# An S4D convolution by matmuls: the spectra's product in a form chosen by block, the skip term by four 32x32 products, a third buffer for one factor of the kernel rows, and an order of the work read from a table

## The chip, the core and the metric

The kernel runs on one core of a Trainium2 chip. The core has five engines with a queue of instructions each: TensorE (PE in the profile, its weight loads apart as PEld), VectorE (DVE), ScalarE (ACT), GpSimd (POOL) and SyncE (SP), which issues transfers here. Each queue runs in its written order and waits at its head by semaphores. The metric is the device time of one execution in microseconds, lower is better.

## The reference

One layer over 2048 tokens of 640 channels: an adaptive layer norm, a long convolution by a diagonal state space model (S4D), a gated sum, a second norm and a SwiGLU feed-forward network (FFN) of 1728 hidden channels.

```python
def _A_ref(u, log_A_real, A_imag, C_real, C_imag, log_dt, D_skip):
    dt = jnp.exp(log_dt)
    A = -jnp.exp(log_A_real) + 1j * A_imag                 # [640, 128]
    C = (C_real + 1j * C_imag) * dt[:, None]
    P = jnp.exp((A * dt[:, None])[:, :, None] * pos)       # pos = 0 .. 2047
    K = 2.0 * jnp.einsum("dn,dnl->dl", C, P).real          # one kernel row a channel
    y = irfft(rfft(u, 2 * L) * rfft(K, 2 * L))[:L]         # along the tokens
    return y + u * D_skip

mod = (_silu(c) @ w_mod).reshape(1, 6, 1, -1)
sa, ca, ga, sb, cb, gb = ...
h = _layernorm(x) * (1 + ca) + sa
x = x + ga * _A_ref(h, ...)
h = _layernorm(x) * (1 + cb) + sb
x = x + gb * ((_silu(h @ w1) * (h @ w3)) @ w2)
```

## The kernel before

**Stages.** The channels are cut into five blocks b = 0 .. 4 of 128. For each block the kernel makes the convolution's kernel rows, transforms them and the normalized input, multiplies the spectra, transforms back and stores the result (`zd`). When all five blocks are done, rows of 128 tokens are read back from `zd` (`iz`, `izb`), the last step of the inverse transform adds them to x (`iy`, `iyb`), and the second norm, the transposes (`tp`) and the FFN follow (`gu` are the first gate and up products, then `acc`, `c`, `X`). The change does not touch the FFN's own code (`ffn`, L1412, and what it calls).

**Kernel rows** (`gen_chunk`, L594; tasks in `gen_tasks`, L1739). A block has eight chunks c of 16 channels, named `g{b}.{c}`. A chunk runs: on POOL a phase `ph` and three sizes z0, z1 (two halves of `yy`) and z2 (half of `xx`), from the tables `p` and the exponents `e` and `late` (made by ACT in `exp_tasks`, L1933, from the products `al` x `j`); on ACT one Abs on `ph` and four sines `tr`; on DVE five products m0 to m4 that complete `yy` and `xx`; on PE 32 matmuls of 32 columns, four side by side in the array (`kps`); on ACT a copy of the result into `ks` (task r); on DVE the sum of the skip term D into position 63 of each row of `ks` (task d, `skip`, L1761). `yy` and `xx` have two buffers each, `kps` one PSUM tile of two halves that alternate, `tr` three PSUM tiles.

**Transforms and product.** A first transform is a task m of eight matmuls into one PSUM bank, eight such tasks a block for the kernel rows (`ps<-wk,ks`) and eight for the input (`ps<-wk,xb`) (`first_tasks`, L1812); its moving matrix `wk` has two zero blocks of 64x64. ACT or DVE copies each bank to `sp` or `sp2`. The second transform makes half tiles i = 0 .. 7 of the spectra, `fh` of the input and `fk` of the kernel, eight matmuls each (`spectra_tasks`, L1850). ACT holds `fh` in SBUF as `hz`. DVE multiplies complex numbers: `fp = fk * re(hz)`, `fk = fk * im(hz)`, both of 512 elements a partition, and then one difference and one sum of 256 (`both`, L1879). Two half tiles make one `fp`, and `inverse` (L1886) makes of it two banks `fz` with two matmuls each, whose copies `zt` go to `zd`.

**The normalized input.** `h_tasks` (L1793) normalizes tokens into `hn` (on ACT or DVE), multiplies and adds rows into `hb` on DVE, stores it (`hs`) and reads it back turned as `xb`.

**The order.** All tasks up to the first hidden tiles are recorded with the tasks that they follow, the rings of buffers that they take and give, and one or two engines that may run them (`Plan`, L168). `place` (L188) then walks the tasks as a list scheduler with modelled durations and delays; ties go by a table `RANKS` of one number a task. The result is the order of each engine's queue. Every instruction passes through a helper that keeps this order (`InOrder`, whose line is L157 for all of them), so the trace tells instructions apart by tile and shape, not by line.

Of the kernel before, what the change touches and what calls it, by code (L numbers as in the profile page):

```python
# [29 lines left out]
EXPS = ((0, 0, 0, 64.0), (0, 1, 0, 1.0), (1, 0, 0, 512.0), (1, 1, 4, 8.0), (1, 2, 0, 8.0))  # L30
# [3 lines left out]
RANKS = """  # L34
# [132 lines left out]

class Plan:  # L168

    LAG = dict(PE=0.2, DVE=0.18, ACT=0.2, POOL=0.15, SP=0.0)
    CHAIN = dict(DVE=0.12, ACT=0.12, POOL=0.07)
# [2002 lines left out]
```

## Time and profile before

| | |
|---|---|
| median of three runs | 973.44 us (972.19 to 976.54) |
| profiled execution | 972.31 us |
| its span | 970.5 us |
| its mean granted TensorE clock | 0.975 |
| DVE, last product of a kernel row ends | 342.5 us |
| PE, last `kps` ends | 346.4 us |
| PE, first `gu` in the chain that ended last | 398.07 us |

Times in the views are microseconds from the start of the span. Rows of groups give the engine, the operation, the result's tile and the operands' tiles (buffer numbers left out), partitions x elements, the count, then busy time and the mean duration in ns, then the idle time of that engine just before them and the engine and tile that ended it. An fp32 matmul leaves two records, so 32 matmuls of `kps` are 64; a few records are missing here and there. In the chain of waits each piece is what the next one waited for.

### The profile page before, as it was taken

How to read it: one execution, taken by the hardware profiler on the slowest of the kernel's cores; microseconds unless marked ns; L12 is line 12 of the kernel's file. 1: busy time of each engine (PE TensorE's matmuls, PEld its weight loads, DVE VectorE, ACT ScalarE, POOL GpSimd, SP SyncE). 2: the span in 40 equal slices, each digit the busy share in tenths (PEclk: the TensorE clock that was granted, in tenths of full speed). 3: DMA queues.
4: the chain of work that ended last, by engine and by line, in shares of the span. 5: the costliest groups of instructions: out<-in, count | busy, mean ns of one | idle time of the engine just before them, and what ended most of it. 6: DMA issues, size and time to landing. Idle time of an engine off the chain costs nothing.

```text
span 970.5 us, 20551 instructions
## 1 busy us (share of the span) xinstructions
PE 859.9 (89%) x7985; PEld 681.8 (70%) x7985; DVE 702.0 (72%) x1395; ACT 546.4 (56%) x1022; POOL 340.5 (35%) x371
## 2 busy tenths in 40 slices
PE   1464787889899997899999999999999999999997
PEld 1132665767778884677777778888788888888775
DVE  7998899999999968886767677557456464645422
ACT  6877788979888851564434455346444344443412
POOL 1797889879799600002111111000011212120000
PEclk9996999999999999799999999999999999999999
DMA  9955453723425268935434422276342322220374
GB/s 218 275 168 191 111 136 95 177 66 106 111 80 152 74 159 206 241 118 182 122 120 139 122 96 68 82 209 194 112 134 64 102 77 86 82 82 28 108 220 133
DMA packets 110506, 127.31 MB, mean 131 GB/s; under 512 B 10568, under 2 KB 90696, under 8 KB 109128
## 3 DMA queue, kind: packets, MB, share of 16 engines
q1 hardware_dynamic: 109032, 125.21, 45.3%
q8 instruction: 63, 1.03, 0.5%
q10 hardware_dynamic: 1376, 0.79, 0.3%
q14 instruction: 35, 0.29, 0.1%
HBM read 95.82 MB, written 30.15 MB: 130 GB/s over the span
## 4 chain that ended last, share of the span: by engine, by line
PE 70%; DVE 17%; ACT 5%; issue 4%; DMA 3%; POOL 1%; SPq 1%; ACTq 0%; DVEq 0%
PE c L157 19%; PE acc L157 18%; PE X L157 12%; PE ps L157 4%; PE gu L157 3%; DVE yy L157 3%; PE kps L157 3%; PE fz L157 2%; PE fk L157 2%; DVE fp L157 2%; PE fh L157 2%; DVE hn L157 2%; DVE xx L157 2%; DVE xb L157 1%; ACT tr L157 1%
## 5 line engine op out<-in xcount | busy, mean ns | idle before, releaser
L157 PE MATMUL acc<-ah,w 128*128 128x512 f32 x560 | 173.2, 395 | 2.4 <-DMA w<-w2d 1.7
L157 PEld LDWEIGHTS acc<-ah,w 128*128 128x128 f32 x560 | 103.7, 188 | 26.4 <-issue 2.1
L157 PE MATMUL acc<-al,w 128*128 128x512 f32 x260 | 102.4, 394 | 0.0
L665 DVE TENSOR_TENSOR wl<-s,wh 128x256 fp32r<-128x256 f32 x92 | 38.9, 423 | 67.5 <-ACT wh L664 67.1
L841 POOL TENSOR_TENSOR s<-wr 128x256 f32<-128x256 f32 x22 | 16.4, 744 | 187.8 <-DMA wr<-in_w 94.8
L157 POOL TENSOR_TENSOR ph<-p,p 128x1024 int32<-128x1024 int32 x40 | 79.2, 1979 | 8.2 <-ACT tr L157 8.0
L664 ACT ACTIVATE wh<-s 128x256 fp32r<-128x256 f32 x92 | 37.6, 410 | 78.5 <-PE X L157 58.1
L157 PE MATMUL kps<-yy,xx 128*32 128x64 f32 x2560 | 51.8, 234 | 28.6 <-DVE xx L157 21.4
L157 DVE TENSOR_TENSOR yy<-yy,tr 128x512 f32<-128x512 f32 (+1 forms) x80 | 75.3, 943 | 1.2 <-ACT tr L157 0.6
L157 PEld LDWEIGHTS kps<-yy,xx 128*32 128x32 f32 x2560 | 45.1, 116 | 38.3 <-issue 22.0
L664 ACT ACTIVATE wh<-wr 128x256 fp32r<-128x256 f32 x92 | 38.4, 418 | 56.0 <-PE X L157 42.3
L842 POOL TENSOR_TENSOR s<-s,wr 128x256 f32<-128x256 f32 x22 | 16.6, 755 | 134.0 <-issue 133.9
L902 ACT ACTIVATE t<-g 128x512 f32<-128x512 f32 x44 | 27.8, 632 | 52.7 <-DVE g L866 52.7
L157 ACT ACTIVATE tr<-ph,hpi 128x512 f32<-128x512 f32 x80 | 54.6, 690 | 4.4 <-DVE xx L157 2.7
L157 PEld LDWEIGHTS acc<-al,w 128*128 128x128 f32 x260 | 48.9, 188 | 10.8 <-DVE al L665 0.3
L871 DVE SCALAR_TENSOR_TENSOR g<-t,g 128x512 f32<-128x512 f32 x48 | 33.7, 702 | 31.3 <-ACT t L902 29.3
L157 POOL TENSOR_TENSOR yy<-e,e 128x512 f32<-128x512 f32 x48 | 52.4, 1109 | 8.8 <-PE kps L157 5.9
L157 DVE TENSOR_TENSOR xx<-tr,xx 128x512 f32<-128x512 f32 x80 | 54.3, 680 | 1.1 <-ACT tr L157 1.1
L157 PE MATMUL ps<-wk,ks 128*64 128x128 f32 x640 | 42.4, 285 | 13.6 <-DVE ks L157 8.9
L157 ACT ACTIVATE tr<-ph 128x512 f32<-128x512 int32 x80 | 47.3, 598 | 12.4 <-DVE yy L157 6.5
L157 PE MATMUL ps<-wk,xb 128*64 128x128 f32 x640 | 46.1, 295 | 6.3 <-ACT sp L157 3.0
L157 PEld LDWEIGHTS ps<-wk,ks 128*64 128x64 f32 x640 | 37.0, 143 | 20.3 <-ACT hn L157 6.6
(448 smaller groups left out, 2379.7 us busy)
## 6 DMA issues: line engine op xcount, KB each, us to landing
w<-w2d SPq DMA_DIRECT2D x42, 640.0 KB, 3.9
wr<-in_w SPq DMA_DIRECT2D x50, 320.0 KB, 3.9
zd<-zt SPq DMA_DIRECT2D x40, 256.0 KB, 2.9
w2d<-w SPq DMA_DIRECT2D x14, 640.0 KB, 3.5
xs<-in_x SPq DMA_DIRECT2D x16, 320.0 KB, 11.3
hs<-hb SPq DMA_DIRECT2D x20, 256.0 KB, 2.5
xb<-hs SPq DMA_DIRECT2D x20, 256.0 KB, 4.9
iz<-zd SPq DMA_DIRECT2D x32, 160.0 KB, 5.0
```

The costliest lines, as they stand in the source:

```text
L157: self.prev = self.k.order(f(*a, **kw), self.prev)
L664: self.nc.scalar.activation(H, v, AF.Copy)
L665: eng.tensor_tensor(Lo, v, H.bitcast(F32), op=ALU.subtract)
L841: eng.tensor_tensor(s[0], u[:, 0:2], u[:, 2:4], op=ALU.add)
L842: eng.tensor_tensor(s[1], s[0], g[:, 0:2], op=ALU.subtract)
L871: V.scalar_tensor_tensor(g, th, 1.0, g, op0=ALU.add, op1=ALU.mult)
L902: tanh = lambda o, i: A.activation(o, i, AF.Tanh, scale=0.5)
```

## The change

**The spectra's product** has a form for each block, `FORM = "AABBC"`. B is the form of before. A is one DVE instruction for a half tile, all four products of 1024 elements a partition, into an `fp` of twice the size; the difference and the sum are left to PSUM, with a third matrix in `wz` and eight matmuls for a tile of `fz` where there were four. C is the one product, then the difference and the sum from SBUF, and gives the bank of `fk` free before these.

**The skip term** is four matmuls of 32x32 with the identity, on top of `kps`; task d and its DVE instruction are gone. Each `kps` is a PSUM tile of its own in a ring of one.

**The first transform** skips the zero blocks of `wk`: eight columns of the input take 32 matmuls in the four quadrants of the array, into two banks; four tasks a block for eight.

**Buffers and tables.** Each third chunk of blocks 0 to 3 takes its `yy` in `x2[0]`, named `x_94` in the trace, which nothing uses until later. The products for the exponents are made in the exponents' own tile, on POOL in all five blocks. `iz` tiles 0 and 1 use `sp2`.

**The order** is a table of task numbers (an apostrophe chooses the second engine) that `sequence` reads and checks against the tasks and the rings; the model is gone. The tasks' durations, now used by nothing, changed too.

```diff
-EXPS = ((0, 0, 0, 64.0), (0, 1, 0, 1.0), (1, 0, 0, 512.0), (1, 1, 4, 8.0), (1, 2, 0, 8.0))
+EXPS = ((0, 0, 0, 64.0), (1, 0, 0, 512.0), (1, 1, 4, 8.0), (1, 2, 0, 8.0), (0, 1, 0, 1.0))
-RANKS = """
--1152 -1540 -1534 -1515 -1509 -1417 -1345 -1436 -1412 -1402 -1385 -1330 -1273 -1351 -1452 -1478 -1480 -1475 -1459 -1510 -1507
...
+ORDER = """
+1 78 80 81 82 83 79 150 2 20 19 21 86 22 23 84 42 41 5 4 43 44 24 25 45 46 14 111 15 16 17 47 18 30 26 8 27 107 48 49 31 100 50 61
...
+FORM = "AABBC"
-    wz = np.tile(np.stack([np.block([c, s]), np.block([-s, c])], 1), (2, 1, 1))
+    wz = np.tile(np.stack([np.block([c, s]), np.block([-s, c]), np.block([-c, -s])], 1), (2, 1, 1))
...
+        for x in ORDER.split():
+            n = names[int(x.rstrip("'"))]
+            engs, _, _, after, _, _, take, give, _, _ = T[n]
+            assert n not in done and done.issuperset(after), n
...
+            out.append((engs[x.endswith("'")], n))
...
+    def in_third(self, b, c):
+        return b < NB - 1 and (8 * b + c) % 3 == 2
+
+    def third(self):
+        return self.x2[0].rearrange("p j d -> p (j d)")[:, :2048].rearrange("p (r d a i) -> p r d a i", r=2, d=self.CD, a=2)
...
-        yy = w.tile([P, 2, C, 2, 32], F32, name=f"yy_{d0}", tag="yy")
+        yy = self.third() if self.in_third(d0 // P, d0 % P // C) else w.tile([P, 2, C, 2, 32], F32, name=f"yy_{d0}", tag="yy")
...
+            for q in range(4):
+                g = slice(32 * q, 32 * q + 32)
+                nc.tensor.matmul(kps.rearrange("p (e b) -> p e b", b=64)[g, :, 63], self.ident[g, g], self.dsk[g, d0 // P, d0 % P // 4:d0 % P // 4 + 4],
+                                 start=False, stop=True, skip_group_check=True, tile_position=(32 * q, 32 * q))
...
-                if b == c == 0:
-                    self.kg = self.psg.tile([P, 2, 256], F32, name="kps", tag="kg", bufs=1)
-                kps[c] = self.kg[:, c % 2]
+                kps[c] = self.psg.tile([P, 256], F32, name=f"kps{b}{c}", tag="kg", bufs=1)
...
-        def skip(c):
-            o = slice(4 * c, 4 * c + 4)
-            V.tensor_add(self.ks[b][:, o, 63], kps.pop(c).rearrange("p (e b) -> p e b", b=64)[:, :, 63], self.dsk[:, b, o])
...
-            for e in range(4):
-                x = self.ks[b][:, 4 * i + e, :] if m else xb[:, :, 4 * i + e]
+            for e in range(8):
+                x = self.ks[b][:, 8 * i + e, :] if m else xb[:, :, 8 * i + e]
                 for r in range(2):
-                    o = pk[i][r * 64:(r + 1) * 64].rearrange("p (v j i f) -> p i j v f", j=4, i=4, f=2)[:, e]
-                    nc.tensor.matmul(o, x, self.wk[:, r, :], start=True, stop=True, tile_position=(0, 64 * r))
+                    for h in range(2):
+                        g = slice(64 * h, 64 * h + 64)
+                        o = pk[i, h][r * 64:(r + 1) * 64].rearrange("p (v j i f) -> p i j v f", j=2, i=8, f=2)[:, e]
+                        nc.tensor.matmul(o, x[g], self.wk[g, r, g], start=True, stop=True, tile_position=(64 * h, 64 * r))
...
+            if form == "B":
+                k = bank[1, i]
+                for r in range(2):
+                    nc.vector.tensor_mul(k if r else prod[i // 2][:, 0, :, o, :].rearrange("p r q d -> p q r d"), k, bc(held[i][:, :, r], 2, 2))
+                return
+            k = bank.pop((1, i)).rearrange("p q r d -> p r (q d)")
+            h = held[i].rearrange("p q r d -> p r (q d)")
+            to = prod[i // 2][:, :, :, o, :].rearrange("p s r q d -> p s r (q d)")
+            nc.vector.tensor_mul(to, bc(k, 1, 2), bc(h, 2, 2))
...
+            terms = ((0, 0, 0), (0, 1, 1), (1, 1, 2), (1, 0, 1))[:2 if last else 4]
...
+            for n, (s, r, w) in enumerate(terms):
                 for f in range(2):
                     g = slice(64 * f, 64 * f + 64)
+                    nc.tensor.matmul(bank["z", j, f], self.wz[g, w, :], p[g, s, r], start=(n == 0), stop=(n == len(terms) - 1), tile_position=(64 * f, 0))
...
+            x[0] = E[0][:, :, 1, :]
             self.eng(e).tensor_tensor(x[0], bc(self.al[:, b], 2, 8), bc(self.j8, 1, P), op=ALU.mult)
```

How the queues stand, at three places. First DVE while the kernel rows of the second block are made, where the products of the first block's spectra stand between the products of the chunks (`yy`, `xx`) and the normalization (`hn`, `hb`). Before:

```order
L157 TENSOR_TENSOR fp_1507<-fk_1482,hz_1473 128x2x2x128
L157 SCALAR_TENSOR_TENSOR yy_1469<-yy_1469,tr_192_1492 128x16x32
L157 TENSOR_TENSOR fk_1482<-fk_1482,hz_1473 128x512
L157 TENSOR_TENSOR fp_1507<-fk_1514,hz_1524 128x2x2x128
L157 TENSOR_TENSOR fp_1507<-fp_1507,fk_1482 128x256 x2
L157 TENSOR_TENSOR fk_1514<-fk_1514,hz_1524 128x512
L157 TENSOR_TENSOR yy_1469<-yy_1469,tr_192_1492 128x16x32
```

Now:

```order
L149 TENSOR_TENSOR fp_1492<-fk_1478,hz_1487 128x4x256
L149 TENSOR_TENSOR xx_1444<-tr_160_1461,xx_1444 128x512
L149 TENSOR_TENSOR hb_1495<-hn,rw 128x512
L149 SCALAR_TENSOR_TENSOR yy_1445<-yy_1445,tr_160_1447 128x16x32
L149 TENSOR_TENSOR hn<-hn,rw 128x512
L149 TENSOR_TENSOR hb_1573<-hn,rw 128x512
L149 TENSOR_TENSOR fp_1492<-fk_1552,hz_1566 128x4x256
```

The four rows of a half tile (two products, a pair of sums) are one row with the product of 1024 elements, and nothing follows it on DVE.

Second PE at the end of the kernel rows, from the last two chunks on. Before:

```order
L157 MATMUL kps<-yy_4463,xx_4462 32x64 x32
L157 MATMUL ps_4787<-wk,ks_4131 64x4x16x2 x8
L157 MATMUL ps_4798<-wk,ks_4131 64x4x16x2 x8
L157 MATMUL kps<-yy_4582,xx_4581 32x64 x32
L157 MATMUL ps_4841<-wk,ks_4131 64x4x16x2 x8
L157 MATMUL ps_4878<-wk,ks_4131 64x4x16x2 x8
L157 MATMUL ps_4892<-wk,ks_4131 64x4x16x2 x8
L157 MATMUL ps_4912<-wk,ks_4131 64x4x16x2 x8
L157 MATMUL fh_4926<-sp,wb 64x128 x8
```

Now (the last two rows alternate, sixteen of each, to the end of the task, and `fh` follows them):

```order
L149 MATMUL kps_5523<-yy_5290,xx_5289 32x64 x32
L149 MATMUL kps_5523<-dsk,ident 32x4 x4
L149 MATMUL kps_5570<-yy_5439,xx_5438 32x64 x32
L149 MATMUL kps_5570<-dsk,ident 32x4 x4
L149 MATMUL ps_5610<-wk,ks_4792 64x2x16x2
L149 MATMUL ps_5611<-wk,ks_4792 64x2x16x2
```

The four rows `dsk,ident` are the skip term. The last two chunks stand side by side, and one task of the first transform stands behind the last of them, where four stood.

Third POOL in the second block. Before, each chunk's sizes go into one of two buffers `yy`:

```order
L157 TENSOR_TENSOR ph_1089<-p_119,p_120 128x1024
L157 TENSOR_TENSOR yy_1091<-late 128x16x32
L157 TENSOR_TENSOR xx_1090<-late 128x512
L157 TENSOR_TENSOR yy_1091<-late 128x16x32
L157 TENSOR_TENSOR ph_1169<-p_119,p_120 128x1024
L157 TENSOR_TENSOR xx_1170<-late 128x512
```

Now the block's first chunk has its sizes in `x_94`, and the product for a later block's exponents is on POOL (its last row here):

```order
L149 TENSOR_TENSOR ph_1087<-p_119,p_120 128x1024
L149 TENSOR_TENSOR x_94<-late 128x16x32
L149 TENSOR_TENSOR xx_1088<-late 128x512
L149 TENSOR_TENSOR x_94<-late 128x16x32
L149 TENSOR_TENSOR ph_1305<-p_119,p_120 128x1024
L149 TENSOR_TENSOR yy_1307<-late 128x16x32 x2
L149 TENSOR_TENSOR xx_1306<-late 128x512
L149 TENSOR_TENSOR ph_1443<-p_119,p_120 128x1024
L149 TENSOR_TENSOR yy_1445<-late 128x16x32 x2
L149 TENSOR_TENSOR ph_1451<-p_119,p_120 128x1024
L149 TENSOR_TENSOR xx_1444<-late 128x512
L149 TENSOR_TENSOR e_122<-al,j_110 128x128x8
```

In these rows the sizes go to three different buffers in turn, and POOL has one instruction of 1024 elements more.

More of the change, by code (lines that the diff above doesn't have):

```diff
@@ L168 @@
 class Plan:
-    LAG = dict(PE=0.2, DVE=0.18, ACT=0.2, POOL=0.15, SP=0.0)
-    CHAIN = dict(DVE=0.12, ACT=0.12, POOL=0.07)
-    NEAR, RATE, LAND, FLY, ISSUE, AWAY, TABLE = 0.1, 235e3, 1.3, 0.7, 0.06, 8, 1.28
     def __init__(self, **rings):
@@ L258, in place @@
+        taken, done, out = {r: [] for r in self.n}, set(), []
+        for x in ORDER.split():
+            n = names[int(x.rstrip("'"))]
+            engs, _, _, after, _, _, take, give, _, _ = T[n]
+            assert n not in done and done.issuperset(after), n
+            for r, y, _ in take:
+                i = len(taken[r]) - self.n[r]
+                assert i < 0 or not uses[r, taken[r][i]], n
+                taken[r].append(y)
             for k in give:
                 uses[k] -= 1
-                given[k] = max(fin + self.LAG.get(e, 0.0), given.get(k, 0.0))
@@ L261, in place @@
-                if not uses[k]:
-                    freed[k] = given[k]
-            for m in nexts[n]:
-                left[m] -= 1
-                if not left[m]:
-                    ready.append(m)
-        assert len(end) == len(T), ("never", [n for n in T if n not in end][:20])
-        return order
-    def run(self):
-        T = self.tasks
-        found = [int(x) for x in RANKS.split()]
-        searched = [n for n in T if n not in self.own]
-        assert len(found) == len(searched)
-        self.order = self.place({n: t[4] for n, t in T.items()} | dict(zip(searched, found)))
-        for s, f, e, n in self.order:
-            if T[n][2]:
-                T[n][2](e)
+            done.add(n)
@@ L282 @@
+            out.append((engs[x.endswith("'")], n))
+        assert len(done) == len(T)
+        return out
+    def run(self):
+        for e, n in self.sequence():
+            if self.tasks[n][2]:
+                self.tasks[n][2](e)
 class K:
@@ L1113, in dst @@
                         return z[u][pr][h * 64:h * 64 + 64]
-                    load(f"iz{u}.{pr}{h}", zv[:, t0:t0 + 2, :cut], dst, 262144, done + ([f"hh{b4}.{i}.m" for i in range(8)] if u > 2 else []))
+                    load(f"iz{u}.{pr}{h}", zv[:, t0:t0 + 2, :cut], dst, 262144, done + ([f"hh{b4}.{i}.m" for i in range(4)] if u > 2 else []),
+                         "inv" if u < 2 else "change")
         def load_up(m):
@@ L1613, in border @@
             self.x2 += [self.fp.tile([P, 4, D], F32, name=f"x2{i}") for i in (2, 3)]
-        plan.add("change", None, 0, change, [f"g{b}.7.p", f"g{b}.7.d"] + [f"h{b}.{i}.x" for i in range(4)], 0, own=True)
+        plan.add("change", None, 0, change, [f"g{b}.7.p", f"g{b}.7.r"] + [f"h{b}.{i}.x" for i in range(4)], 0, own=True)
         self.tail_tasks(border, cut)
@@ L1787, in gen_tasks @@
                     give=[("tr", n + f"s{(0, 0, 1, 3, 4)[i]}")])
-            add(n + "p", "PE", 1.1, lambda c=c: ch[c][4](), [n + f"m{i}" for i in range(5)], t + 3,
-                take=[("kg", 1)], give=[("yy", n + "z0"), ("xx", n + "z2")])
-            add(n + "r", "ACT", .27, lambda c=c: rows(c), [n + "p"] + ([f"k{b - 1}.{i}.m" for i in range(8)] if b else ["exp0", "q0.t0", "q1.t0"]), t + 3, give=[("kg", n + "p")])
-            add(n + "d", "DVE", .1, lambda c=c: skip(c), [n + "r"] + (["dsk"] if b == 0 else []), t + 3, give=[("kg", n + "p")])
+            add(n + "p", "PE", 1.25, lambda c=c: ch[c][4](), [n + f"m{i}" for i in range(5)] + (["dsk"] if b == 0 else []), t + 3,
+                take=[("kg", 1)], give=[(yy, n + "z0"), ("xx", n + "z2")])
+            add(n + "r", "ACT", .27, lambda c=c: rows(c), [n + "p"] + ([f"k{b - 1}.{i}.m" for i in range(4)] if b else ["exp0", "q0.t0", "q1.t0"]), t + 3, give=[("kg", n + "p")])
     def h_tasks(self, b):
@@ L1855, in spectra_tasks @@
         bank, prod, held = {}, {}, {}
-        four = lambda x: x.rearrange("p (q r d) -> p q r d", q=2, r=2)
+        form = FORM[b]
+        last = form != "A"
+        four = lambda x: x.rearrange("p (r q d) -> p q r d", q=2, r=2)
         def of(m, i):
@@ L2035, in early_tasks @@
         for b in range(4):
-            add(f"x{b}", "SP", 0, lambda b=b: load_xs(b), [], next(lp), dma=[327680] * 4, take=[("xs", 1)])
+            add(f"x{b}", "SP", 0, lambda b=b: load_xs(b), [], next(lp), dma=[360000] * 4, take=[("xs", 1)])
         for k in range(5):
@@ L2086, in scale @@
             self.h_rs = self.rsqrt(self.gp, self.h_ss, NJ, "h", (self.h_nm, 1.0), 1.0 / D, [t[:, i * NJ:(i + 1) * NJ] for i in range(2)])
-        add("hscale", "DVE", 6.5, scale, [f"mean{b}" for b in range(4)] + [f"sq{b}{j}" for b in range(4) if b not in W["stat_v"] for j in range(4)], W["stat"](4), take=[("f2", 1)])
+        add("hscale", "DVE", 5.5, scale, [f"mean{b}" for b in range(4)] + [f"sq{b}{j}" for b in range(4) if b not in W["stat_v"] for j in range(4)], W["stat"](4), take=[("f2", 1)])
         add("hscalef", None, 0, None, ["hscale"], give=[("f2", "hscale")])
@@ L2095, in rows_begin @@
             A.activation(m[:96, 384:], pm[0][:96, 384:], AF.Copy)
-        add("m", "ACT", .9, rows_begin, ["mr4"], 20, take=[("hz", 4)])
+        add("m", "ACT", .6, rows_begin, ["mr4"], 20, take=[("hz", 4)])
         pr = {}
@@ L2117, in fold @@
             V.tensor_mul(self.rB, self.rB, self.rows[2])
-        add("fold", "DVE", 1.6, fold, [f"rw{g}" for g in range(4)], 22, port=True)
+        add("fold", "DVE", 3.2, fold, [f"rw{g}" for g in range(4)], 22, port=True)
         add("wb", "SP", 0, lambda: nc.sync.dma_start(self.wb, self.t_wb), ["fold", "mr4", "lat1", "turn1"], 60, dma=[2097152])
```

270 lines of the change are left out of this document (121 added, 149 removed), and 80 rows, old and new, of tables (ORDER, RANKS).

## The prediction

> **What bounds the kernel now.** I read the page first: its busy totals, its slices, its chain.
>
> ```profile
> PE 859.9 (89%) x7985; PEld 681.8 (70%) x7985; DVE 702.0 (72%) x1395; ACT 546.4 (56%) x1022; POOL 340.5 (35%) x371
> PE   1464787889899997899999999999999999999997
> DVE  7998899999999968886767677557456464645422
> POOL 1797889879799600002111111000011212120000
> PE 70%; DVE 17%; ACT 5%; issue 4%; DMA 3%; POOL 1%; SPq 1%; ACTq 0%; DVEq 0%
> ```
>
> A slice is 24 us. In the first fourteen (to about 340 us) DVE stands at 8 or 9 and PE below it for long; behind them PE alone stands at 9. Averages hide two programs, so the second view is busy time by stretches (us, then PE, PEld, DVE, ACT, POOL busy with their counts, granted clock, DMA share, GB/s): the convolution's generation of rows, its end, the first gated tiles, and the FFN's rest.
>
> ```profile
> 105.50:342.50 237.00, 207.26 (x4226) 173.90 (x4228) 226.74 (x418) 198.72 (x339) 202.51 (x198) 0.97 0.42 110
> 342.50:398.10 55.60, 46.35 (x594) 34.31 (x583) 42.92 (x128) 20.09 (x38) 0.63 (x1) 0.89 0.81 197
> 448.90:970.50 521.60, 511.87 (x2284) 407.71 (x2283) 299.16 (x593) 220.68 (x447) 62.51 (x84) 1.00 0.37 114
> 171.20:236.40 65.20, 56.01 (x1120) 46.81 (x1118) 62.77 (x119) 56.21 (x95) 56.69 (x57) 0.95 0.43 114
> 291.50:342.50 51.00, 49.78 (x1052) 42.15 (x1050) 48.86 (x88) 42.68 (x76) 39.43 (x34) 1.00 0.42 115
> ```
>
> From 448.9 us on PE is busy 511.87 of 521.60 us, and the change doesn't touch that code: 522 us stand. From 105.5 to 342.5 us DVE is busy 96% and PE 87%. So DVE sets this stage, with PE behind it; in its last block (291.5 to 342.5) PE is busy 49.78 of 51.00 and the two are level. What is taken from DVE is worth its full size only as long as PE and POOL have room.
>
> **The change part by part.** Instructions on DVE overlap a little, so I cost them by the distance between starts, from the timeline (start, duration, engine, instruction):
>
> ```profile
> 303.37 0.15 DVE L157 TENSOR_TENSOR ks<-kps,dsk 128x4 f32<-128x4 f32 x1
> 303.69 1.22 DVE L157 TENSOR_TENSOR yy<-yy,tr 128x1024 f32<-128x1024 f32 x1 [0.17 <-ACT tr L157]
> 304.83 0.68 DVE L157 TENSOR_TENSOR fp<-fk,hz 128x512 f32<-128x512 f32 x1
> 305.44 0.68 DVE L157 TENSOR_TENSOR xx<-tr,xx 128x512 f32<-128x512 f32 x1
> 306.59 0.17 DVE L157 TENSOR_TENSOR ks<-kps,dsk 128x4 f32<-128x4 f32 x1 [0.47 <-ACT ks L157]
> 306.67 0.69 DVE L157 TENSOR_TENSOR fk<-fk,hz 128x512 f32<-128x512 f32 x1
> 307.98 0.74 DVE L157 TENSOR_TENSOR fp<-fp,fk 128x256 f32<-128x256 f32 x2
> 308.64 0.68 DVE L157 TENSOR_TENSOR fp<-fk,hz 128x512 f32<-128x512 f32 x1
> ```
>
> 512 elements take 0.60 us of the queue (304.83 to 305.44), 1024 take 1.14 (303.69 to 304.83), a pair of 256-element sums 0.66 (307.98 to 308.64). *Products.* A half tile i of the spectra costs 0.60 + 0.60 + 0.66 = 1.86 us on DVE now. Form A, in blocks 0 and 1, is one product of 1024: no row has one with a factor in PSUM. From below it is the 1.14 of `yy<-yy,tr`, from above two products of 512, 1.20; I take 1.16, so 0.70 less for each of 16 half tiles: -11.2 us. Form C, in block 4, makes 1.86 into 1.14 + 0.66: next to nothing.
>
> The other edits on DVE, by groups of equal instructions up to 342.5 us (busy and mean ns, then idle time before them and its releasers):
>
> ```profile
> L157 DVE TENSOR_TENSOR ks<-kps,dsk 128x4 f32<-128x4 f32 x38 | 5.7, 157 | 5.6 <-PE kps L157 3.1 <-ACT ks L157 1.3 <-ACT hn L157 1.1
> L157 DVE TENSOR_SCALAR hn<-xq,rs_y_h,rs_n_h 128x128 f32<-128x128 f32 x44 | 18.1, 412 | 1.2
> L157 DVE COPY sp<-ps 128x512 f32<-128x512 f32 x19 | 12.7, 682 | 2.5 <-PE ps L157 2.3
> L157 DVE COPY zt<-fz 128x512 f32<-128x512 f32 x5 | 3.4, 684 | 0.8 <-PE fz L157 0.7
> L157 DVE TENSOR_TENSOR xs_al<-al,j 128x1024 f32<-128x1024 f32 x1 | 2.8, 2835 | 0.0
> L157 DVE TENSOR_TENSOR ks<-al,j 128x1024 f32<-128x1024 f32 x1 | 1.2, 1216 | 0.0
> ```
>
> The skip adds go: of their 0.157 some 0.10 is the queue's own (306.59 to 306.67 is the least), so 38 make -3.8, and their 5.6 us of idle can go too. The two exponent tables go to POOL: -4.0. The table moves 16 pieces of the first normalization to ACT, -16 x 0.40 = -6.4, and back to DVE 12 copies of the first transform and 5 of the inverse: 17 x 0.61 = +10.4. Sum on DVE: -11.2 - 3.8 - 4.0 - 6.4 + 10.4 = **-15.0 us**, before any idle time.
>
> *PE* pays for it. Its groups up to 346.4 us, two rows of its weight loads, and pieces of the chain of waits (start, length):
>
> ```profile
> L157 PE MATMUL kps<-yy,xx 128*32 128x64 f32 x2560 | 51.8, 234 | 28.6 <-DVE xx L157 21.4 <-POOL xx L157 2.9 <-ACT sp L157 2.4
> L157 PE MATMUL ps<-wk,xb 128*64 128x128 f32 x640 | 46.1, 295 | 6.3 <-ACT sp L157 3.0 <-ACT zt L157 1.4 <-DVE fp L157 1.4
> L157 PEld LDWEIGHTS kps<-yy,xx 128*32 128x32 f32 x2560 | 45.1, 116 | 38.3 <-issue 22.0 <-POOL xx L157 4.0 <-POOL yy L157 3.0
> L157 PEld LDWEIGHTS ps<-wk,xb 128*64 128x64 f32 x640 | 42.5, 220 | 10.9 <-ACT sp L157 4.4 <-issue 3.0 <-ACT zt L157 2.3
> ```
> ```profile
> 306.13 1.06 PE fh L157 x16
> 307.19 0.91 PE fk L157 x16
> 325.08 1.10 PE kps L157 x61
> 326.18 1.92 PE fz L157 x8
> 345.29 1.10 PE kps L157 x61
> 346.39 3.64 PE ps L157 x64
> 364.36 0.74 DVE fp L157 x2
> ```
>
> An fp32 matmul leaves two records. *Inverse.* Four more matmuls for each of 8 tiles of form A: 8 x 1.92 = +15.4 us (326.18), in the second and third block, where PE has room (busy 56.01 of 65.20 in 171 to 236 us). *Skip term.* Four matmuls are 8 records; at the 1.10 us of 64 `kps` records they are 0.14, from above four whole `kps` durations, 0.94. A change of shape shows at 306.13: `fh` behind `kps` takes 1.06 and the `fk` after it 0.91, so 0.15. I take 0.15 for each chunk, near the low end, since the four go to different quarters of the array: 34 chunks after 105.5 us, +5.1; with a change of shape on either side of them it is 0.30, +5 more. The Trainium skill, "TensorEngine Tiling (Array Packing)", Key Properties, says that a change of tiling mode drains the engine; the trace agrees with its 0.15, and by that rule PE's sum below would be +14. *First transform.* Eight columns now take 32 quadrant matmuls, 64 records like a `kps` task, where they took 32 records of twice the width. For the kernel rows that was 3.64 / 2 = 1.82 us (346.39); at the `kps` rate it is 1.10, or 2.2 if the 64-column load, twice as wide, is what counts. I take 1.10 (the streamed width, 64, is that of `kps`): 4 tasks x 4 blocks x -0.72 = -11.5. For the input's half the loads are the longest, 220 ns against 116, and fill 42.5 of 46.1 us; I leave it at its present cost, bounds -15 (at the `kps` rate) and +2. Sum on PE: +15.4 + 5.1 - 11.5 = **+9**, so 216 us of work in a stage that would last 222.
>
> *POOL and ACT.* The third buffer goes against POOL's waits, shown for 34 to 342 us with total, number and longest; the tables cost POOL two rows more:
>
> ```profile
> POOL yy L157 <- PE kps L157: 14.9, 11, 3.9
> POOL ph L157 <- ACT tr L157: 8.0, 6, 3.0
> L157 POOL TENSOR_TENSOR al<-al,j 128x1024 f32<-128x1024 f32 x3 | 5.9, 1971 | 0.0
> L157 ACT ACTIVATE ks<-kps 128x256 f32<-128x256 f32 x38 | 14.3, 379 | 10.5 <-PE kps L157 9.3 <-DVE ks L157 0.8
> L157 ACT ACTIVATE ph<-ph 128x1024 f32<-128x1024 int32 x40 | 42.2, 1055 | 0.4
> ```
>
> +2 x 1.97 = +3.9 us in POOL's queue, hidden by its 34 idle us (202.51 busy of 237), which shrink by the 15 the stage is to lose and, at best, by these 14.9. One `kps` buffer for two makes each `kps` wait for ACT's copy of the chunk before; a copy is 0.38, and ACT was idle before it waiting for PE (9.3 us), so it follows its `kps` at once and PE has other tasks in between. I take 0, from above the copy and its signal each time, some 0.6 x 34 = 20 us.
>
> *Sum.* The stage ends at 342.5 - 15.0 + 0.5 = 328: the idle before the skip adds (5.6) goes, and I give as much and 0.5 more to a PE and a POOL that are nearly full. Its end: behind the last `kps` stand one new transform task, not four old ones (1.10 for 3.64, -2.5); the last two `kps` are neighbours and share a buffer, +0.6; form C moves two sums off PSUM (such a pair stands in the chain at 364.36), -0.5. So -2.4. The profiled execution took 972.31 (span 970.5 and 1.8 around it): 972.31 - 14.5 - 2.4 = 955.4. It lay 1.1 below the median of the runs, 973.44, so I predict **956**.
>
> **The rivals.**
> *POOL takes over* (to 966). Its waits for `kps` were 11 with up to 3.9 us; if the third buffer, used for each third chunk alone, takes away half (7.5) and the tables add 3.9, its last phase moves by 4 us, not 15. With the tail: -6.4. Against it: POOL was busy only 85% of the stage.
> *PE takes over through weight loads* (to 969). If a 64-column load lasts as long with half the rows, a new task is 64 x 0.034 = 2.2 us, the kernel rows' half costs +6, not -11.5, the input's +2; PE then has 207 + 15 + 5 + 8 = 235 us, and the stage ends near 340: -2.5, tail -1. For it: `PEld` is busy 45.1 of `kps`'s 51.8. Against: 128-row loads of 64 columns go in 1.82 / 32 = 0.057 with N = 128, so streaming sets that row. The Trainium skill has the rule for this rival: "TensorE: Matmul & The Clock Gate", LDWEIGHTS (loading the stationary operand), counts a load by its columns and not by its rows.
> *Slower: the single `kps` buffer* (987). `kps` waits at the head of PE's queue until ACT has come to the copy, with transforms and inverses behind it; ACT is busy 84% of the stage (198.72 of 237). PE has 222 - 216 = 6 us to spare; a wait of w for 34 chunks adds 34w - 6. The whole gain of 17 is gone from w = 0.68 on, and at 1.1 us it is +31 - 17 = +14: 987. For it: a `ph` row of 1.055 us may stand ahead of such a copy. Against: the 9.3 us above.
> *No gain* (972). A new order puts waits where DVE was freed; the transfers between the last spectrum and the first inverse row are untouched either way.
>
> **How the numbers follow.** Forecast 0.56 (its own range 947 to 963: products 1.20 and skip at 0.30 above, the input's half at the `kps` rate and the idle gone below). POOL 0.11, PE 0.12, single buffer 0.12, no gain 0.09. A measurement here tells about 0.5% (4.9 us) from no change. Faster: 0.56 + 0.11, half of PE's, and 0.02 of no gain: 0.75. Same: the other half and 0.04: 0.10. Slower: 0.12 + 0.03 = 0.15. The range goes from 940, below the forecast's own by the rest of PE's and DVE's idle, to 974, which leaves out the buffer's case and some ends.
>
> **What would show it.** Products of 1024 at about 1.2 us and no `ks<-kps,dsk` on DVE; `fz` chains of 3.8 us in two blocks; a quadrant task of the kernel rows near 1.1 us (2.2 speaks for PE's rival); POOL's waits on `kps` well below 14.9; the last `kps` done near 332 (before: 346.4) and `gu` some 17 us earlier. `kps` waiting for ACT's `ks` by more than 0.6 us a chunk would make the prediction wrong, as would PE idle time that DVE no longer explains.

## The result

The changed kernel is slower by 0.7%.

| kernel | median us | runs | ratio to before, 95% interval |
|---|---|---|---|
| before | 972.9 (971.1 to 976.9) | 9 | |
| changed | 981.7 (975.3 to 984.7) | 9 | 1.0074 (1.0044 to 1.0103) |
| predicted | 956 (940 to 974) | | |

The profiled execution of the changed kernel took 983.58 us, 11.3 more than that of before. Its page, the busy totals, two of the slices and the transfers of instructions (queue, kind, number, MB, share):

```profile
PE 871.1 (89%) x9649; PEld 685.0 (70%) x9649; DVE 686.3 (70%) x1292; ACT 548.4 (56%) x1026; POOL 344.2 (35%) x376
PE   1355787899998979699999999999999999999997
DVE  7889789889996958888677767657465564646322
q8 instruction: 76, 1.25, 0.5%
```

Of the page before the last of these rows read

```profile
q8 instruction: 63, 1.03, 0.5%
```

DVE has 15.7 us less to do, as planned. PE's matmul records rose from 7985 to 9649, and 1.25 MB of instructions are fetched, 16 KB at a time, for 1.03. That these blocks are PE's is read from the numbers: 13 blocks more for 1664 more matmul and as many more load records of PE come to 64 bytes a record, and so do all 76 for all records, within 1%.

Where the time went is seen by three ends. The last `kps` ends at 361.5 us (before 346.4), the first `gu` starts at 410.6 (397.7), and the rest takes 571.2 us (572.8). So the loss lies in the stage that makes the kernel rows: 15 us later, where the prediction had 14.5 earlier. Busy time by stretches in that stage, the changed kernel (columns as in the prediction: length, PE, PEld, DVE, ACT, POOL, clock, DMA, GB/s):

```profile
0.00:354.70 354.70, 267.09 (x6580) 207.45 (x6580) 306.64 (x511) 278.78 (x490) 278.05 (x287) 0.92 0.51 134
105.50:361.50 256.00, 226.17 (x5837) 183.47 (x5838) 217.81 (x329) 196.82 (x338) 201.85 (x198) 0.93 0.40 109
```

and the kernel before, to the end of its last product of the kernel rows:

```profile
0.00:342.50 342.50, 252.87 (x4907) 200.63 (x4909) 319.47 (x600) 277.04 (x488) 274.09 (x282) 0.95 0.52 140
```

DVE's work up to that product fell by 12.8 us, yet its idle time rose from 23.0 to 48.1. PE was busy 226.17 of 256.0 us from 105.5 on: 30 us idle; and its clock, granted at 0.93, is worth up to 18 us more (7% of 256). The kernel before, from 105.5 us to its last `kps` (the sum of four stretches, whose granted clocks were 0.96, 0.92, 1.00 and 1.00), was idle for 30 us too:

```profile
sum 240.90, PE 211.16 PEld 177.44 DVE 226.90 ACT 200.73 POOL 202.51; mean PE 52.79 PEld 44.36 DVE 56.73 ACT 50.18 POOL 50.63
```

So it isn't the amount of idle time that changed but what PE waited for, and its clock. The waits, in total, number and longest, from 34 us to the end of the stage, changed kernel (some rows left out):

```profile
PE kps L149 <- issue: 9.7, 8, 3.3
PE kps L149 <- DVE yy L149: 9.6, 1, 9.6
PE kps L149 <- DVE xx L149: 7.8, 5, 3.6
PE ps L149 <- issue: 5.7, 6, 3.1
PE kps L149 <- POOL ph L149: 5.1, 2, 4.6
PE kps L149 <- ACT ks L149: 3.9, 1, 3.9
PE fh L149 <- issue: 1.3, 1, 1.3
PE prow L149 <- issue: 0.8, 1, 0.8
```

and of before, the two largest and those for issue:

```profile
PE kps L157 <- DVE xx L157: 21.4, 9, 12.1
PE ps L157 <- DVE ks L157: 8.9, 3, 5.7
PE kps L157 <- issue: 1.4, 2, 0.9
PE fh L157 <- issue: 1.3, 1, 1.3
```

"Issue" is idle time that no semaphore explains: 17.5 us, before 2.7. PE's timeline shows what it is like (start, length, count, and in brackets the idle time before):

```profile
351.26 1.97 PE L149 MATMUL ps<-wk,ks 64*64 64x64 f32 x117 [0.90 <-issue]
353.16 0.42 PE L149 MATMUL kps<-yy,xx 128*32 128x64 f32 x11
356.91 1.08 PE L149 MATMUL kps<-yy,xx 128*32 128x64 f32 x53 [3.33 <-issue]
357.92 0.24 PE L149 MATMUL kps<-dsk,ident 32*32 32x4 f32 x8
358.71 1.96 PE L149 MATMUL kps<-yy,xx 128*32 128x64 f32 x64 [0.55 <-issue]
```

PE stops for 3.33 us in the middle of one `kps` task, behind 11 of its 64 records. All operands of that task were there, since the first 11 records had run. In that gap the trace has one block of 16 KB of instructions in flight, from 354.11 to 355.43 us, and PE goes on 1.48 us behind its landing. This is so for nearly all of them: from 100 us to the last `kps` the changed kernel has 14 pieces of issue, and 13 end 1.2 to 1.5 us behind the landing of such a block. A stall can cost twice, as the stretch of another and the one that follows it show:

```profile
294.80:298.00 3.20, 0.01 (x1) 0.00 (x0) 1.67 (x3) 0.00 (x0) 2.84 (x2) 0.89 0.94 191
300.70:304.30 3.60, 3.60 (x13) 1.18 (x8) 1.22 (x1) 1.92 (x4) 3.29 (x8) 0.52 0.00 0
```

PE ran nothing from 294.8 to 298.0, and behind it the clock is granted at about half: the inverse of 8 records took 3.65 us there, where it takes 1.92.

The new operations themselves, by groups:

```profile
L149 PE MATMUL ps<-wk,xb 64*64 64x64 f32 x1280 | 46.3, 291 | 2.3 <-DMA xb<-hs 0.8 <-issue 0.7 <-DVE hb L149 0.4
L149 PE MATMUL ps<-wk,ks 64*64 64x64 f32 x1280 | 28.0, 236 | 7.5 <-issue 4.9 <-DVE sp L149 1.2 <-ACT sp L149 0.6
L149 PE MATMUL kps<-dsk,ident 32*32 32x4 f32 x320 | 10.2, 182 | 0.4 <-issue 0.4
L149 DVE TENSOR_TENSOR fp<-fk,hz 128x1024 f32<-128x1024 f32 x16 | 19.5, 1220 | 3.6 <-PE fk L149 2.7 <-ACT hz L149 0.8
```

A quadrant task of the kernel rows is 28.0 / 20 = 1.40 us, of the input 46.3 / 20 = 2.32, a skip term 10.2 / 40 = 0.26.

### The profile page after: what moved, and what is told of

Its sections match the earlier page's. It is cut to its first block, busy times and chain, and to the rows that moved or that the text cites. A ratio compares the mean times of both kernels' runs of the same rounds, so it can differ in the third digit from the quotient of the medians.

```text
span 981.8 us, 23787 instructions
## 1 busy us (share of the span) xinstructions
PE 871.1 (89%) x9649; PEld 685.0 (70%) x9649; DVE 686.3 (70%) x1292; ACT 548.4 (56%) x1026; POOL 344.2 (35%) x376
## 3 DMA queue, kind: packets, MB, share of 16 engines
q8 instruction: 76, 1.25, 0.5%
## 4 chain that ended last, share of the span: by engine, by line
PE 56%; DVE 2%; ACT 2%; DMA 2%; issue 1%; SPq 0%; POOL 0%; ACTq 0%; DVEq 0%
PE c L149 19%; PE acc L149 18%; PE X L149 12%; PE gu L149 2%; PE iy L149 1%; DMA zd<-zt 1%; PE tp L149 1%; PE to L149 1%; DMA w<-w2d 1%; DMA izb<-zd 1%; PE fh L149 1%; PE fz L149 1%; PE ps L149 1%; PE fk L149 1%; PE kps L149 1%
## 5 line engine op out<-in xcount | busy, mean ns | idle before, releaser
L149 PE MATMUL kps<-yy,xx 128*32 128x64 f32 x1920 | 41.8, 240 | 32.8 <-DVE yy L149 9.6
L149 PEld LDWEIGHTS kps<-yy,xx 128*32 128x32 f32 x1920 | 35.8, 120 | 42.9 <-issue 18.0
L149 DVE TENSOR_TENSOR yy<-yy,tr 128x512 f32<-128x512 f32 (+1 forms) x60 | 56.8, 948 | 9.9 <-ACT tr L149 9.1
L774 POOL TENSOR_TENSOR s<-s,wr 128x256 f32<-128x256 f32 x22 | 16.6, 753 | 133.8 <-issue 133.8
L149 PE MATMUL fz<-fp,wz 64*128 64x512 f32 x224 | 59.5, 657 | 0.5 <-DVE fp L149 0.5
L597 DVE TENSOR_TENSOR wl<-wr,wh 128x256 fp32r<-128x256 f32 x92 | 40.3, 439 | 15.1 <-ACT wh L596 15.0
L149 PE MATMUL ps<-wk,xb 64*64 64x64 f32 x1280 | 46.3, 291 | 2.3 <-DMA xb<-hs 0.8
L149 DVE TENSOR_TENSOR fp<-fk,hz 128x1024 f32<-128x1024 f32 (+1 forms) x40 | 40.2, 1007 | 11.5 <-PE fk L149 10.5
## 6 DMA issues: line engine op xcount, KB each, us to landing
zd<-zt SPq DMA_DIRECT2D x40, 256.0 KB, 3.0
hs<-hb SPq DMA_DIRECT2D x20, 256.0 KB, 2.6
xb<-hs SPq DMA_DIRECT2D x20, 256.0 KB, 4.9
```

What stands on the lines that cost most here:

```text
L149: self.prev = self.k.order(f(*a, **kw), self.prev)
L597: eng.tensor_tensor(Lo, v, H.bitcast(F32), op=ALU.subtract)
L774: eng.tensor_tensor(s[1], s[0], g[:, 0:2], op=ALU.subtract)
```

## The experiments

Three theories. *Code*: PE's queue runs dry, since its instructions come in blocks by the same transfer engines as the data, and the change makes it go through them faster. *Work*: PE became the bound by form A and the skip term. *Order*: the table makes the waits. Each verdict names the median and the ratio to before with its interval.

**1. The wide first transform** (`ps_wide`). The changed kernel; the first transform's matmuls are those of before again, in the new tasks, banks and order, and the copies out of the banks follow their layout.

```diff
+WIDE = (0, 1)
...
+            if m in WIDE:
+                for e in range(8):
+                    x = self.ks[b][:, 8 * i + e, :] if m else xb[:, :, 8 * i + e]
+                    for r in range(2):
+                        o = pk[i, e // 4][r * 64:(r + 1) * 64].rearrange("p (v j i f) -> p i j v f", j=4, i=4, f=2)[:, e % 4]
+                        nc.tensor.matmul(o, x, self.wk[:, r, :], start=True, stop=True, tile_position=(0, 64 * r))
+                return
...
+            if m in WIDE:
+                o = o[:, :, :, 16 * i + 8 * h:16 * i + 8 * h + 8]
...
```

> The changed kernel (981.7 us) with the first transform back in its wide form: sixteen matmuls of 128 rows and 128 columns a task instead of thirty-two in quadrants, in the same tasks, banks and order. 640 matmuls fewer in PE's queue, but for the kernel rows some 0.6 us more PE work a task (20 tasks, +12 us). Theory code: PE's queue runs dry because its instructions, fetched in blocks of 16 KB, come too late when it goes through them fast and the transfers are busy; the idle time of PE that the profile puts down to issue falls from 17.5 us to under 6, and the time falls to 966 to 974 in spite of the added work. Theory work: PE is simply the bound, by form A and the skip term; the time rises to 988 to 994. Theory order: the table's order makes the waits; within 3 us of 982.

Measured: 965.0 us, 0.9925 (0.9909 to 0.9940). Its stage, and two parts of its middle, and PE's idle time put down to issue:

```profile
105.50:343.30 237.80, 222.92 (x4688) 184.76 (x4684) 215.72 (x331) 197.12 (x339) 201.63 (x198) 0.99 0.42 113
165.00:225.00 60.00, 59.21 (x1204) 47.75 (x1202) 54.63 (x76) 50.44 (x86) 53.27 (x52) 1.00 0.34 91
225.00:285.00 60.00, 59.47 (x1295) 50.45 (x1295) 54.62 (x91) 50.67 (x85) 55.20 (x55) 1.00 0.25 65
```
```profile
PE ps L150 <- issue: 1.6, 2, 1.2
PE kps L150 <- issue: 1.2, 1, 1.2
PE prow L150 <- issue: 0.8, 1, 0.8
PE fh L150 <- issue: 0.3, 1, 0.3
```

*Code* holds: with more matmul work and 640 fewer matmuls the kernel is 17 us faster, issue falls from 17.5 to 3.9 us, the clock is granted at 0.99 for 0.93. PE's account from 105.5 us to the last `kps`, with half of the time at half clock counted as lost:

| kernel | length, us | idle | lost to the clock | work at full clock |
|---|---|---|---|---|
| before | 240.9 | 30 | 7 (half of 13.7) | 204 |
| changed | 256.0 | 30 | 17 (half of 33.5) | 209 |
| wide | 237.8 | 15 | 2 (half of 3.4) | 221 |

Against the wide form the quadrants save some 12 us of work and cost 30: 15 of idle time, of which 12.5 are issue (15.6 for 3.1 from 105.5 us on), and 15 of clock. Against before, 13 us of issue came in and as much waiting for other engines went; the end is later by 10 us of clock and 5 of work.

Not all of the clock's part is traced to late instructions. Of the 33.5 us at half clock, 13 follow the three long stalls for instructions and 10 follow two waits for ACT, of 2.5 and 3.9 us; the rest stands behind shorter gaps. The wide kernel has the same two waits, and 3.4 us at half clock behind them.

**2. The two halves apart** (`hh_wide`, `k_wide`): the same edit for the input alone (`m == 0`), and for the kernel rows alone (`m == 1`).

> The changed kernel (981.7 us) with the wide form for the input's first transform alone; the kernel rows keep the quadrants. A quadrant task of the input took 2.2 us and two wide tasks of before 2.1, so PE's work is equal within 2 us in all; its queue is 320 matmuls shorter. Theory code: the idle time of PE put down to issue falls from 17.5 us to 6 to 11, the time to 968 to 976. Theory work: within 3 us of 982, since the work is the same. If the kernel rows' quadrants alone make the fast stretch that runs dry, issue stays above 13 us and the time above 978.

> The changed kernel with the wide form for the kernel rows alone; the input keeps the quadrants. Against the kernel with both wide (965.0 us) this has 320 matmuls more in PE's queue, at the same PE work (2.2 us for a quadrant task of the input, 2.1 for two wide ones). Theory code: the added code costs by itself, 970 to 977, with issue idle of PE above 5 us against 3.9. Theory work: 964 to 968, as with both wide.

Measured: `hh_wide` 969.6 us, 0.9966 (0.9948 to 0.9984); `k_wide` 974.1 us, 1.0005 (0.9986 to 1.0024). So 320 matmuls of the input cost 12 us on top of the other quadrants and 9 by themselves, though the input's quadrants take 46.3 us of PE against 44.0 for the wide form. Issue is 8.7 us in the first:

```profile
PE kps L150 <- issue: 5.8, 4, 2.5
PE ps L150 <- issue: 1.8, 1, 1.8
PE prow L150 <- issue: 0.8, 1, 0.8
PE fh L150 <- issue: 0.3, 1, 0.3
```

In `k_wide` it is only 4.6 us, below the 5 that was expected, and the time came all the same. In its trace idle time (15 us) and work (220) are those of `ps_wide`, and the last `kps` ends 6.3 us later, at 349.6: the difference is the clock. The stretches around its one long stall for instructions show a part of it:

```profile
106.60:109.20 2.60, 0.06 (x1) 0.00 (x0) 0.33 (x1) 0.00 (x0) 0.91 (x1) 0.85 0.98 400
109.20:111.00 1.80, 1.79 (x17) 1.67 (x19) 0.00 (x0) 1.39 (x3) 0.00 (x0) 0.50 1.01 319
111.00:113.00 2.00, 2.00 (x22) 1.90 (x18) 0.69 (x1) 1.32 (x3) 1.58 (x1) 0.50 0.94 275
113.00:115.00 2.00, 2.00 (x59) 1.76 (x58) 1.65 (x3) 0.00 (x0) 2.00 (x3) 0.50 0.08 20
```

PE stood still for 2.6 us and then ran at half clock to 115. Half-clock stretches between 105.5 us and the last `kps` add up to 17 us in `k_wide`, 3.4 in `ps_wide`, 33.5 in the changed kernel. But only 6.8 of the 17 us stand behind this stall, the other 10 behind the two waits for ACT. Why those waits cost more clock here than in `ps_wide` stays open.

**3. Transfers beside a stall** (`iz_late`): the changed kernel, with eight loads of 256 KB (and four tasks queued behind them) moved in the order table behind the store `z4.0.o1`; PE's instructions are the same.

> The changed kernel with the loads of the first two inverse rows and the loads queued behind them moved in SP's queue behind the last block's second store, so that the four transfers of 256 KB that start at 353.4 us start some 20 us later. If a fetch of PE's instructions stands behind such transfers, the 3.3 us stall in the last chunk but one shrinks to 0.4 to 1 us, the last product of a kernel row on PE ends 2 to 3 us earlier (361.5 before), and the stall may come back where the loads now are. If the fetch is late by itself, the stall stays at 3 us or more. The end of the program says nothing here, since the loads come late for the inverse rows.

Measured, in one profiled execution: the stall of 3.33 us is 1.13, at the same record:

```profile
353.53 0.42 PE L157 MATMUL kps<-yy,xx 128*32 128x64 f32 x11
355.09 1.08 PE L157 MATMUL kps<-yy,xx 128*32 128x64 f32 x53 [1.13 <-issue]
```

The last `kps` ends at 358.8, 2.7 us earlier. The block that PE waits for is in flight from 352.73 to 353.72 us here, before the stall begins, and from 354.11 to 355.43 in the changed kernel: without the transfers that began at 353.44 us it starts earlier and takes 0.99 us for 1.32. That is what *code* expects, but one pair of executions doesn't show how much of the stall was the transfers' doing: the stall of 1.26 us at 248.00, where nothing was moved, is 2.96 us in this execution, and issue in all is 16.4 us for 17.5. 1.1 us stay without transfers in any case. The end of the program, 995.2 us (1.0226, 1.0193 to 1.0258), is that of the late loads.

**4. The same instructions with the old kernel** (`b_split`): before, each matmul of the first transform cut in two.

```diff
-                    nc.tensor.matmul(o, x, self.wk[:, r, :], start=True, stop=True, tile_position=(0, 64 * r))
+                    for h in range(2):
+                        nc.tensor.matmul(o[:, 2 * h:2 * h + 2], x, self.wk[:, r, 64 * h:64 * h + 64], start=True, stop=True, tile_position=(0, 64 * r))
```

> The kernel before (972.9 us) with each matmul of the first transform cut into two of 64 columns, still with 128 rows: the same products in the same order, 640 matmuls more in PE's queue. Theory code: PE's idle time put down to issue, 2.7 us before, rises above 10 us in the long stage and the time by 5 to 15 us. Theories work and order: the second loads cost PE some tenths of a us a task, the time rises by less than 4 us and issue stays below 5 us, unless a task of 32 matmuls is longer than 1.3 us in its rows, which would make it work.

Measured: 1008.1 us, 1.0368 (1.0350 to 1.0385). No clean test, as its expectation feared:

```profile
L157 PE MATMUL ps<-wk,xb 128*64 128x64 f32 x1280 | 84.8, 291 | 5.1 <-ACT zt L157 1.5 <-DVE fp L157 1.4 <-DMA xb<-hs 1.2
L157 PE MATMUL ps<-wk,ks 128*64 128x64 f32 x1280 | 47.9, 233 | 17.5 <-DVE ks L157 8.4 <-issue 8.3 <-DVE sp L157 0.8
```

Issue did rise (8.3 us in one row, 10.6 in the stage, for 2.7), but the input's half went from 46.1 to 84.8 us of PE: with half the columns streamed for each load a load still takes 66 ns, for 72 before, so its time goes by the number of loads. These 39 us of added work would be enough for the 35 us of added time, so the run can't part the theories.

**5. What is worth what, form A** (`form_b`: the changed kernel with B's arithmetic inside the one task of blocks 0 and 1; `wide_b`: the same on `ps_wide`; `wide_aaa`: `ps_wide` with two result buffers and A in block 2 too).

```diff
+INSIDE = (0, 1)
...
-            if form == "B":
+            if form == "B" or b in INSIDE:
...
+                if b in INSIDE:
+                    both(i)
...
-            terms = ((0, 0, 0), (0, 1, 1), (1, 1, 2), (1, 0, 1))[:2 if last else 4]
+            terms = ((0, 0, 0), (0, 1, 1), (1, 1, 2), (1, 0, 1))[:2 if last or b in INSIDE else 4]
```

> The changed kernel with the arithmetic of form B in blocks 0 and 1, inside the same one task: two products and two sums on DVE, four matmuls for a tile of fz. PE loses 8 x 1.92 = 15.4 us, DVE gains 16 x 0.7 = 11 us, PE's queue loses 32 matmuls only. Theory work: PE was the bound, so the time falls by 6 to 12 us to 970 to 976. Theory code: PE still stalls for its instructions as often, and DVE is longer: 980 to 990, issue idle of PE still above 13 us. Theory order: within 4 us of 982.

> The kernel with the wide first transform (965.0 us) and, besides, the arithmetic of form B in blocks 0 and 1: PE -15.4 us, DVE +11 us. In the wide kernel PE is busy 59.2 of 60 us from 165 to 225 and 59.5 of 60 from 225 to 285. Theory work: with the instructions there in time PE's work is the bound, and form A costs more there than it gives: 956 to 962. Rival: DVE becomes the bound again as soon as it has its sums back: 965 to 975.

> Wide first transform and two result buffers (963.9 us), with form A's arithmetic in block 2 too: PE +7.7 us, DVE -5.6 us. If PE is the bound from 225 to 343 us: 967 to 972. If DVE still is, as the run with form B in blocks 0 and 1 (972.8 for 965.0) suggests: 959 to 963.

Measured: `form_b` 989.7 us, 1.0177 (1.0144 to 1.0209), with 14.1 us of issue; `wide_b` 972.8 us, 1.0002 (0.9983 to 1.0021); `wide_aaa` 971.1 us, 0.9985 (0.9972 to 0.9999). Form A is worth 8 us in blocks 0 and 1, with the many stalls or with few, so its work on PE isn't the cause of the loss. For `wide_b` the first case, by *work*, was wrong and the rival came: with A, PE is busy 59.2 and 59.5 of 60 us; without it (`wide_b`, from 165 to 225 us, in an execution of 978.5 us, 5.7 above its median)

```profile
165.00:225.00 60.00, 49.51 (x1066) 42.65 (x1065) 56.44 (x95) 47.30 (x80) 46.91 (x49) 0.97 0.36 97
```

DVE is the fuller one at 56.4. The two stand so near that either choice meets a bound, and in block 2 (`wide_aaa`) it is PE's:

```profile
225.00:285.00 60.00, 59.72 (x1212) 48.40 (x1210) 46.47 (x62) 47.44 (x80) 50.81 (x51) 1.00 0.22 55
```

**6. The skip term** (`no_skip`: the changed kernel without it; `skip_one`: one matmul of 128x128 for the four; `wide_one`: the same on `ps_wide`).

```diff
-            for q in range(4):
-                g = slice(32 * q, 32 * q + 32)
-                nc.tensor.matmul(kps.rearrange("p (e b) -> p e b", b=64)[g, :, 63], self.ident[g, g], self.dsk[g, d0 // P, d0 % P // 4:d0 % P // 4 + 4],
-                                 start=False, stop=True, skip_group_check=True, tile_position=(32 * q, 32 * q))
+            nc.tensor.matmul(kps.rearrange("p (e b) -> p e b", b=64)[:, :, 63], self.ident, self.dsk[:, d0 // P, d0 % P // 4:d0 % P // 4 + 4],
+                             start=False, stop=True, skip_group_check=True)
```

> The changed kernel without the four matmuls of the skip term (the term D is left out of the result). 160 matmuls fewer in PE's queue and about 0.25 us less PE time for each of 40 chunks. Theory work: PE is the bound, -6 to -10 us, 972 to 976. Theory code: a fetch or two fewer in the stage and some 0.1 us a chunk, -2 to -6 us, 976 to 980. Theory order: within 2 us of 982.

> The changed kernel (981.7 us) with the skip term as one matmul of 128x128 with the whole identity for each chunk in place of four of 32x32: 120 matmuls fewer in PE's queue. With the wide first transform the same edit gave +1.7 us, so PE's own time isn't shorter by it. Theory code: the queue is shorter where it is fetched too slowly, issue idle falls by 2 to 6 us and the time to 974 to 980. Theory work: 980 to 985, as without the edit.

> The kernel with the wide first transform (965.0 us) and the skip term as one matmul of 128x128 with the whole identity for each chunk in place of four of 32x32: 120 matmuls fewer in PE's queue. If the four cost by their number, 0.1 us less of PE a chunk and -2 to -5 us, 960 to 963. If the change of shape is what costs, within 1.5 us of 965.

Measured: `no_skip` 974.9 us, 1.0019 (0.9995 to 1.0042); `skip_one` 981.6 us, 1.0105 (1.0062 to 1.0148); `wide_one` 966.7 us, 0.9935 (0.9911 to 0.9959). The first, 6.8 us less than the changed kernel, lies in the 972 to 976 us of *work* and below the 976 to 980 of *code*: the time of the skip term on PE does count. It takes out instructions as well, and the trace has issue at 13.8 us for 17.5 and half clock at 26.0 for 33.5, so it parts the theories badly. The second lies in the range of *work* too and missed that of *code*, though issue fell by the 5.7 us that *code* expected. What the expectation left out is that one large matmul takes PE longer than the four:

```profile
L149 PE MATMUL kps<-dsk,ident 128*128 128x4 f32 x80 | 16.6, 278 | 0.0
```

It takes 16.6 us against 10.2, so 6.4 us of work came in as 120 matmuls went out (issue 11.8 us, from 17.5), and the time stayed. In `wide_one` it takes 16.4 us against 9.7, and the time rose by 1.7. So both count, PE's work and the number of its instructions.

**7. The buffer, the order, the tail.** `wide_kg2` has two alternating result buffers on `ps_wide`; `wide_tail` adds quadrants for the kernel rows of block 4 alone; `old_ops` has all operations of before in the new order (wide, form B, two buffers, the skip add on DVE behind ACT's copy).

> The kernel with the wide first transform (965.0 us) and two alternating buffers for the kernel rows' result, as in the kernel before, in place of one. PE waited 4.5 us for ACT's copy in two places there. The single buffer as the main cost: -8 us or more, to 957 or less. The single buffer as a small cost: 0 to -3 us, 962 to 965.

> Wide first transform and two result buffers (963.9 us), with quadrants only for the kernel rows of the last block: 4 tasks of 1.4 us in place of 1.95, the last one alone on the chain to the end, and 64 matmuls more. Theory code: the saving of 2 us is kept if PE's queue doesn't run dry there, 961 to 964; if it does, in the stretch in which the inverse's rows are loaded, 965 to 968. Theory work: 961 to 963.

> The changed kernel's order, third buffer and exponent products with every operation of before: wide first transform, form B in blocks 0 and 1, two alternating result buffers, the skip term added on DVE right behind ACT's copy. It is the order by itself, against before at 972.9 us. If the table's order is as good as the planner's for these operations: 970 to 976. If the order is tied to the new operations and hurts the old ones: 978 to 990, with DVE waiting for ACT ahead of the skip adds. If the order is itself the gain: below 968.

Measured: `wide_kg2` 963.9 us, 0.9905 (0.9880 to 0.9930), the fastest of all; `wide_tail` 964.8 us, 0.9926 (0.9903 to 0.9949), no gain; `old_ops` 984.3 us, 1.0126 (1.0094 to 1.0158). The last has its loss on DVE:

```profile
DVE ks L151 <- ACT ks L151: 18.5, 15, 3.7
```

That wait comes from where I put the skip add, so the run shows that this order doesn't suit that operation, and not what the order is worth by itself. That stays open.

## Why the prediction was wrong

**The failed step** is the sum on PE, "so 216 us of work in a stage that would last 222", by the 6 us that it left beside the work, and behind it the pricing of each new matmul by its duration alone ("at the 1.10 us of 64 `kps` records they are 0.14", "64 records like a `kps` task"). The work itself came out about as summed: 209 us at full clock, and the 7 us lost at half clock that the base of 207 already held, make 216. But PE was idle for 30 us and not 6, 15.6 of them issue and the rest waits for the other engines, and the clock took 10 us more than in the base.

What was missing is that PE must also be given its instructions: the change puts 832 matmuls more into its queue (two records each, 9649 for 7985), most of them short and side by side. Experiments 1 and 2 show that the number of matmuls costs time: with fewer of them the kernel is faster, though PE has 12 us more work in the one and nearly equal work in the other. The landings of the blocks show that the stalls end with the instructions' coming. Two sizes stay open: how much of a block's lateness comes from data transfers (experiment 3 points to them, in one stall), and how much of the lost clock comes from late instructions (13 of 33.5 us at half clock follow their long stalls directly). And 6 us were too few even without late instructions: the wide kernel, with 3 us of issue, is idle for 12 us more, behind ACT, DVE and POOL.

**What bounds the kernel**: right. DVE's work fell by 12.8 us (15.7 in `ps_wide`) for 15.0 predicted, products at 1.22 us. But PE was nearer than I treated it: in `ps_wide` it is busy 99% from 165 to 285 us, and that is why even with few stalls the stage gains 3 us and not 14.5. By the prediction's own sum with the transform left as it was (207 + 15.4 + 5.1 = 228 us) PE would have been the bound, and it was busy for 223.

**The terms of PE's work** were sized well, the skip term too low. At full clock 117 records of the kernel rows' quadrants took 1.97 us (at 351.26), so 1.08 for the 64 of a task, predicted 1.10; a skip term took 0.24 (at 357.92) for 0.15. The averages above, 1.40, 2.32 and 0.26, hold the half-clock stretches too: a `kps` task that takes 1.1 us took 1.96 at 358.71.

**The rivals.** *PE takes over* came true in its end and not by its mechanism: a quadrant task takes 1.08 us and not the 2.2 of weight loads; the changed kernel's PE was late more than loaded. The *single buffer*, my only slower case, is worth 1.1 us on the wide kernel (`wide_kg2`), not 14. *POOL* did not take over: its waits for `kps` went from `yy` (14.9 to 5.4 us) to `xx` (1.0 to 10.5), so they moved and none went away. The tail came out as forecast in direction: from the last `kps` to the end 620.3 us for 624.1.

## What to carry to other kernels

Count instructions as a cost of their own: where a change cuts work into more and shorter matmuls, compare how many blocks of instructions the engine must fetch in the densest stretch, and what the transfer engines carry then. Idle time "issue" in the middle of a task, with all operands present, is the sign; look for it before asking which semaphore is late. And when two engines are both nearly full (here DVE was busy 96% of the stage and PE 87%), a gain on the one is worth only what the other has free, stalls included.

## What the runs showed of the hardware

A block of PE's instructions is 16 KB in the trace; 76 of them, 1.25 MB, serve 9649 matmul and 9649 load records, so one lasts for some 128 matmul records, or about 2.3 us of `kps` tasks (72 records in 1.27 us). PE goes on 1.2 to 1.5 us behind the landing of the block that it waits for. With no data transfer beside it (DMA share 0.00 at 181.76, 185.69 and 339.53 us) PE stood for 0.5 to 0.6 us in the changed kernel, and for 1.13 in `iz_late`; beside transfers it stood for up to 3.3 in the changed kernel.

Behind each stall of 2.4 us or more from 105.5 us on, whatever it waited for, the changed kernel's PE clock was granted at 0.50 for 3.4 to 6.8 us. It isn't so each time: behind 2.96 us at 247.72 in `iz_late` and 2.50 at 127.09 in `ps_wide` it stayed at 1.00. The Trainium skill, "TensorE: Matmul & The Clock Gate", What's actually happening, says that the clock has two states, full and half, set by activity in windows of about 3.4 us; the runs agree, with steps of 3.41 us. That a stall for instructions is enough to bring the lower state was new to me.
